# Two queues for the K and V loads of a decode attention kernel: each load split by columns, the second half issued by ScalarE

## The chip, the cores and the metric

One core of a Trainium2 chip. The time is device microseconds (us) of one execution of the whole kernel, from inputs in the chip's main memory to the output in it. Three runs of the kernel before took 1362.27, 1363.26 and 1363.33 us; the median is 1363.26.

The engines named here: PE (TensorE, matrix products), DVE (VectorE), ACT (ScalarE), POOL (GpSimd) and SP (SyncE, which here only issues transfers). Transfers run on 16 transfer (DMA) engines that all queues share. A transfer is cut into packets, here one for each partition's row, and every transfer engine carries the rows of 8 of the 128 partitions and then one 4-byte packet that counts up the transfer's semaphore.

## The reference

One token is decoded. Attention over a cache of 16384 positions in 32 heads, beside a gated GELU block, both on the normalised input, all in float32:

```python
def _A_ref(x, k_cache, v_cache, wq, wo):              # H, Dh = 32, 128; D = 576
    q = (x @ wq).reshape(B, Sq, H, Dh).transpose(0, 2, 1, 3)
    scores = jnp.einsum("bhqd,bhkd->bhqk", q, k_cache) * (Dh ** -0.5)
    p = _softmax(scores, axis=-1)                       # 16384 keys a head
    o = jnp.einsum("bhqk,bhkd->bhqd", p, v_cache)
    return o.transpose(0, 2, 1, 3).reshape(B, Sq, H * Dh) @ wo

def _B_ref(x, w_gate, w_up, w_down):                    # 576 -> 4608 -> 576
    g, u = x @ w_gate, x @ w_up
    return (_gelu(g) * u) @ w_down

x = A_x
xn = _layernorm(x, axis=-1)
return x + _A_ref(xn, ...) + _B_ref(xn, ...)
```

K and V of one head are 16384 x 128 floats each, 8.39 MB; 32 heads make 537 MB of the 587.6 MB that the kernel reads.

## The kernel before

A head's K lies on the 128 partitions as 128 keys a partition, in one row of 65536 B (N * DH floats); so does its V. There are three places of that size: `kt[0]` (in the profile kb) for the even heads' K, `kt[1]` (ka) for the odd heads' K, and one `vt` for V.

The kernel opens with the projections: wq, w_gate and w_up are loaded and multiplied on DVE row by row. Then every engine runs its own program for the heads, and they meet through semaphores that `take` waits for and counts down again (line 118).

- DVE (`scores`, line 367) waits for K, multiplies it in place by the broadcast query (line 356), sums over the 128 columns of each key (line 360), releases the K place with `s_kf` (line 362) and forms the maximum over all keys (lines 363 and 365).
- PE (`on_pe`, line 332) makes the broadcast query of the next head but one, transposes and spreads the maximum, waits for the exponentials and for V (`s_v`, line 341), and multiplies both in 32 products (line 344). After ACT has copied the sums it brings them into a column (line 349), and the first of these products releases V's place with `s_vf` (line 351).
- ACT (`on_act`, line 385), one loop over pairs of heads, copies the query, takes the exponentials (line 395), copies PE's sums (line 397) and the head's column (line 399).
- SP (`on_sp`, line 417) issues the loads, all on its one queue, in the order K of head 2, V of head 1, K of head 3, V of head 2 and so on: each waits until its place is released.

K of head 0 comes in two loads by columns (lines 411 and 412), every other K and V in one. After SP's loop follow, on the same queue and in this order: the first part of w_down into kb's place (`wd0`, 28 blocks of 576, line 427, when head 30's K is done with), V of head 31 (line 428, when V's place is released by head 30), the second part of w_down (line 429) and the first part of wo (both when head 31's K is done with), and the second part of wo into kb's place again (line 445), which waits for `k_w0`, the last of the 28 multiply-adds of wd0.

At the end DVE adds w_down's blocks into `wacc` (line 253, 28 from wd0, then 8), normalises the heads' outputs (lines 462 to 469), adds 11 blocks of wo, and sums its part with that of PE (line 495); PE does the rest of wo, ACT and DVE copy the row out and SP writes it.

Of the kernel before, what the change touches and what calls it, by code (L numbers as in the profile page):

```python
# [8 lines left out]
AF = mybir.ActivationFunctionType  # L9
# [5 lines left out]
H, SK, DH = 32, 16384, 128  # L15
D, DF = 576, 4608
N = SK // P
DJ = 4
DM = P * DJ
SCALE = DH**-0.5  # L20
# [18 lines left out]
class Plan:  # L39
# [24 lines left out]
    def dma(self, e, out, in_, *deps, sem=None):  # L64
        sem = sem or self.sem(f"d{len(self.count)}")
        return self.op(e, lambda g: g.dma_start(out, in_), *deps, sig=sem, by=16)
# [51 lines left out]
def take(g, sem, n=1):  # L118
    g.wait_ge(sem, n).then_inc(sem, -n)  # L119
# [12 lines left out]
def plan(nc, pl, x, k_cache, v_cache, wq, wo, wg, wu, wd, out):  # L132
    op, dma = pl.op, pl.dma
    kv = k_cache.rearrange("b h (p n) d -> (b h) p (n d)", p=P)
    vv = v_cache.rearrange("b h (p n) d -> (b h) p (n d)", p=P)
# [8 lines left out]
    def small(name, shape, where=None):  # L144
        if where is None:
            size = 4
            for n in shape[1:]:
                size *= n
            where = place[name] = top[0]
            top[0] += -(-size // 32) * 32  # L150
            assert top[0] <= S0, (name, top)
        return nc.alloc_sbuf_tensor_at(name, shape, F32, offset=where).ap()

    def big(name, floats, where):
        assert where + 4 * floats <= 3 * SLOT
        return nc.alloc_sbuf_tensor_at(name, [P, floats], F32, offset=S0 + where).ap()
# [8 lines left out]
    qb = [small(f"qb{i}", [P, DH]) for i in range(2)]  # L165
    sc = [small(f"sc{i}", [P, N]) for i in range(2)]
    pm, nm, nb, pe = small("pm", [P, 1]), small("nm", [1, 1]), small("nb", [P, 1]), small("pe", [P, N])
    ls, o4 = small("ls", [P, H + 1]), small("o4", [P, 512])
    oall, oT = small("oall", [P, H + 1]), small("oT", [P, WT])
# [15 lines left out]
    kt = [big("kb", N * DH, B), big("ka", N * DH, A)]  # L185
    vt = big("vt", N * DH, C)
# [4 lines left out]
    def banks(*shapes):  # L191
        with ExitStack() as s:
            return [s.enter_context(nc.psum_tensor(n, [P, b, 512], F32)).ap() for n, b in shapes]

    (pw,) = banks(("pw", 3))
    pt, pb, pc, pqb, po, acc, fin = banks(("pt", 1), ("pb", 1), ("pc", 1), ("pqb", 1), ("po", 1), ("acc", 2), ("fin", 1))
    px = pc[:, 0, :]

    s_hs, s_pm, s_nm, s_p, s_o4, s_v = (pl.sem(n) for n in ("hs", "pm", "nm", "p", "o4", "v"))
    s_pq, s_pt, s_pb, s_pv, s_pc = (pl.sem(n) for n in ("pq", "pt", "pb", "pv", "pc"))  # L200
    s_qb, s_ol, s_kf, s_vf, s_d, s_a = (pl.sem(n) for n in ("qb", "ol", "kf", "vf", "d", "a"))
    s_kh, s_aside = pl.sem("kh"), pl.sem("aside")
    s_k = [pl.sem(f"k{i}") for i in range(2)]
# [44 lines left out]
    s_r, s_w, s_h0, s_q0 = (pl.sem(n) for n in ("r", "w", "h0", "q0"))  # L248
# [12 lines left out]
    def rows(w, t, d, parts, between=None):  # L261
        n = w[0].shape[-1] // 2
        r = [u[:, j * n : (j + 1) * n] for u in w for j in range(2)]
        op("dve", lambda g: g.tensor_scalar(r[0], r[0], xp[:, :1], None, op0=ALU.mult), d[0], k_x)
        add(r[1], r[1], xp[:, 1:2], r[0])
        made = between and between()
        for i in range(2):
            c = r[1][:, i * n // 2 : (i + 1) * n // 2]
            add(c, t, xt[:, i : i + 1], c, d[1])
        k_s = add(r[2], r[2], xp[:, 2:3], r[1], d[2])  # L270
        v = [u.rearrange("p (i c) -> p i c", i=4) for u in (r[3], r[2])]
        for lo, hi, to in parts:
            k = add(bv[:, :, to : to + hi - lo], v[0][:, :, lo:hi], xp[:, 3:4], v[1][:, :, lo:hi])
        pads = [op("pool", lambda g, lo=lo, hi=hi: g.memset(bv[:, :, lo:hi], 0.0), k_s)
                for lo, hi in ((384, SEL), (SEL + 384, 2 * SEL), (2 * SEL + 256, 3 * SEL)) if len(parts) > 1]
        pl.then("dve", [s_r], k, *pads[-1:])
        return k_s, k, made
# [25 lines left out]
    def pick(g, h):  # L303
        return g.activation(hsel, hcol[:, bass.ds(h, 1)].to_broadcast([P, P]), AF.Copy)  # L304
# [5 lines left out]
    u_k, _, k_g = rows(uw, ut, d_u, [(0, DF // 4, 0)], lambda: select(gu[:, 0], SEL, 32, 2))  # L310
# [11 lines left out]
    v = sel[:, : 32 * FT].rearrange("p (r t) -> p r t", r=32)  # L322
    k = op("pool", lambda g: g.tensor_mul(v, v, m32[:, :32].unsqueeze(2).to_broadcast([P, 32, FT])), k, c_m32)
    for r in (16, 8, 4, 2, 1):
        o = v[:, :r, :] if r > 1 else u_.unsqueeze(1)
# [6 lines left out]
    def on_pe(g):  # L332
        with g.Fori(0, H):
            take(g, s_hs)
            g.matmul(pqb[:, 0, :DH], hsel, qsel, start=True, stop=True).then_inc(s_pq, 1)  # L335
            take(g, s_pm)
            g.transpose(pt[:1, 0, :P], pm, ident).then_inc(s_pt, 1)  # L337
            take(g, s_nm)
            g.matmul(pb[:, 0, :1], ones[:1, :], nm, start=True, stop=True).then_inc(s_pb, 1)  # L339
            take(g, s_p)  # L340
            take(g, s_v, 16)
            for k in range(0, N, 4):
                q = 32 * (k // 4 % 4)
                m = g.matmul(po[q : q + 4, 0, :], pe[:, k : k + 4], vt[:, k * DH : (k + 4) * DH],  # L344
                             start=k < 16, stop=k >= N - 16)
            m.then_inc(s_pv, 1)
            take(g, s_o4)
            for j in range(4):
                m = g.matmul(pc[:, 0, :1], o4[:, j * DH : (j + 1) * DH], m32[:, j : j + 1], start=j == 0, stop=j == 3)  # L349
                if j == 0:  # L350
                    m.then_inc(s_vf, 1)
            m.then_inc(s_pc, 1)

    def products(g, i, n=(0, N)):
        kd = kt[i].rearrange("p (n d) -> p n d", d=DH)[:, n[0] : n[1], :]
        g.tensor_mul(kd, kd, qb[i].unsqueeze(1).to_broadcast([P, n[1] - n[0], DH])).then_inc(s_d, 1)  # L356
        take(g, s_d)
# [7 lines left out]
        g.tensor_reduce(nm, pt[:1, 0, :P], axis=AX.X, op=ALU.max, negate=True).then_inc(s_nm, 1)  # L365

    def scores(g, i):
        take(g, s_k[i], 16)
        take(g, s_qb)
        products(g, i)  # L370
        sums(g, i)

    def on_dve(g):
# [7 lines left out]
        with g.Fori(0, H // 2 - 1):  # L381
            for i in range(2):
                scores(g, i)

    def on_act(g):
        with g.Fori(0, H, 2) as h2:
            for i in range(2):
                h = h2 + i
                take(g, s_pq)
                g.activation(qb[1 - i], pqb[:, 0, :DH], AF.Copy).then_inc(s_qb, 1)  # L390
                pick(g, h + 2).then_inc(s_hs, 1)
                take(g, s_pb)
                g.activation(nb, pb[:, 0, :1], AF.Copy, scale=SCALE).then_inc(s_a, 1)  # L393
                take(g, s_a)
                g.activation(pe, sc[i], AF.Exp, bias=nb, scale=SCALE, accum_out=ls[:, bass.ds(h, 1)]).then_inc(s_p, 1)  # L395
                take(g, s_pv)
                g.activation(o4, po[:, 0, :], AF.Copy).then_inc(s_o4, 1)  # L397
                take(g, s_pc)
                g.activation(oall[:, bass.ds(h, 1)], pc[:, 0, :1], AF.Copy).then_inc(s_ol, 1)

    pl.call("pe", on_pe)
    pl.call("dve", on_dve)
    pl.call("act", on_act)

    def load_k(h, *deps):
        dma("sp", kt[h % 2], kv[h], *deps, sem=s_k[h % 2])

    def load_v(h):
        dma("sp", vt, vv[h], (s_vf, 1) if h else (s_w, 3), sem=s_v)

    dma("sp", kt[0][:, : N // 2 * DH], kv[0][:, : N // 2 * DH], g_k, sem=s_kh)
    dma("sp", kt[0][:, N // 2 * DH :], kv[0][:, N // 2 * DH :], sem=s_k[0])
    load_k(1, u_k)
    load_v(0)
    two = [c.rearrange("(m t) p f -> t m p f", t=2) for c in (kv, vv)]

    def on_sp(g):
        with g.Fori(0, H // 2 - 1) as m:
            for i in range(2):
                take(g, s_kf)  # L420
                g.dma_start(kt[i], two[0][i, bass.ds(m + 1, 1)].rearrange("o p f -> (o p) f")).then_inc(s_k[i], 16)
                take(g, s_vf)
                v = two[1][1, bass.ds(m, 1)] if i == 0 else two[1][0, bass.ds(m + 1, 1)]
                g.dma_start(vt, v.rearrange("o p f -> (o p) f")).then_inc(s_v, 16)

    pl.call("sp", on_sp)
    d_wd0 = dma("sp", wd0, wdv[:, : WD1 * D], (s_kf, 1))
    load_v(H - 1)
    d_wd1 = dma("sp", wd1, wdv[:, WD1 * D :], (s_kf, 2))
    k_o = s_ol, H  # L430

# [12 lines left out]
    for n in WO_CUTS:  # L444
        w, base, dep = (wo0, 0, (s_kf, 2)) if lo < WO1 else (wo1, WO1, k_w0)
        c = w[:, (lo - base) * D : (lo - base + n) * D]
# [3 lines left out]
        if lo == WO1:  # L450
            last = wo.rearrange("(s r t) f -> t r s f", s=2, t=WT)[WT - 1]
            for r in [b + j for b in (0, 32) for j in range(4)]:
                to = aside[r : r + 29 : 4].rearrange("r (s f) -> r s f", s=2)
                d_aside = dma("sp", to, last[r : r + 29 : 4, :, LEFT:], dep, sem=s_aside)
    assert len(d_wo) == WT - 2
    for t, a, b in ((WT - 2, LEFT, D), (WT - 2, 0, LEFT), (WT - 1, 0, LEFT)):
        c = wo1[:, (t - WO1) * D + a : (t - WO1) * D + b]
# [12 lines left out]
    for t in ON_DVE:  # L470
        for i, c in enumerate((oT[: P // 2, WT - 1 :], o31) if t == ASIDE else ()):
            to = o_sum[: P // 2, LEFT:]
# [35 lines left out]
    to = osb.rearrange("o a f -> o (a f)")  # L508
    c = op("act", lambda g: g.activation(to[:, LEFT:], third, AF.Copy), k2)
# [31 lines left out]
```

## Time and profile before

| | |
|---|---|
| median of three runs | 1363.26 us (1362.27 to 1363.33) |
| span of the profiled execution, first to last instruction | 1360.5 us |
| DVE busy | 1243.5 us (91%) |
| PE busy | 391.3 us (29%) |
| ACT busy | 66.9 us (5%) |
| transfer engines busy (SP's queue) | 99.8% |
| read from main memory | 587.60 MB, 432 GB/s over the span |

The profiled execution is known by its span; what lies around it in the device time is the 2.8 us between the span and the median of the runs, if it ran like them.

How the rows further down are read. A row of the timeline has the start and the duration in us, the engine, the line of the kernel, the operation, out<-in by the program's names, shapes and count, and in brackets the idle time of the engine before it and what ended it (DVEq is DVE's own sequencer, waiting at a semaphore). SPq is SP issuing a transfer. A row of landings has out<-in, the issuing queue, the count, the KB of each where they are given, and the median us from issue to landing. A row that begins with q1, q8 or q14 counts a hardware queue's packets that start in the given window: packets, MB, and the time that these packets took as a share of 16 engines in the window. In a narrow window one packet's time is therefore share x window x 16. q1 is SP's queue; q8 and q14 bring instructions.

### The profile page before, as it was taken

How to read it: one execution, taken by the hardware profiler on the slowest of the kernel's cores; microseconds unless marked ns; L12 is line 12 of the kernel's file. 1: busy time of each engine (PE TensorE's matmuls, PEld its weight loads, DVE VectorE, ACT ScalarE, POOL GpSimd, SP SyncE). 2: the span in 40 equal slices, each digit the busy share in tenths (PEclk: the TensorE clock that was granted, in tenths of full speed). 3: DMA queues.
4: the chain of work that ended last, by engine and by line, in shares of the span. 5: the costliest groups of instructions: out<-in, count | busy, mean ns of one | idle time of the engine just before them, and what ended most of it. 6: DMA issues, size and time to landing. Idle time of an engine off the chain costs nothing. (4 is left out here: it accounts for less than half of the span.)

```text
span 1360.5 us, 6992 instructions
## 1 busy us (share of the span) xinstructions
PE 391.3 (29%) x2650; PEld 122.4 (9%) x2650; DVE 1243.5 (91%) x228; ACT 66.9 (5%) x234; POOL 36.0 (3%) x25
## 2 busy tenths in 40 slices
PE   0211233333211333333222333332223333322136
PEld 0000011001000111100000111010001111000011
DVE  7999999999988888898888888998888889988888
ACT  0000000000000000000000000000000000000000
POOL 0063000000000000000000000000000000000000
PEclk9655666666556666666556666655666666655667
DMA  9999999999999999999999999999999999999998
GB/s 405 429 437 432 434 447 441 432 432 432 434 432 434 432 432 432 435 451 435 432 432 432 434 432 434 432 432 432 441 447 434 432 432 434 432 434 432 431 432 374
DMA packets 12870, 587.63 MB, mean 432 GB/s; under 512 B 1474, under 2 KB 1986, under 8 KB 2756
## 3 DMA queue, kind: packets, MB, share of 16 engines
q1 hardware_dynamic: 12866, 587.60, 99.8%
q8 instruction: 1, 0.02, 0.0%
q10 hardware_dynamic: 2, 0.00, 0.0%
q14 instruction: 1, 0.01, 0.0%
HBM read 587.60 MB, written 0.00 MB: 432 GB/s over the span
## 5 line engine op out<-in xcount | busy, mean ns | idle before, releaser
L344 PE MATMUL po<-vt,pe 128*4 128x512 f32 x2048 | 291.8, 733 | 611.5 <-PEq L119 611.5
L356 DVE TENSOR_TENSOR kb<-kb,qb 128x16384 f32<-128x16384 f32 (+1 forms) x17 | 277.3, 16314 | 31.8 <-DVEq L119 31.8
L356 DVE TENSOR_TENSOR ka<-ka,qb 128x16384 f32<-128x16384 f32 x16 | 275.6, 17226 | 32.1 <-DVEq L119 32.1
L360 DVE TENSOR_REDUCE sc<-kb 128x128 f32<-128x16384 f32 x16 | 275.5, 17220 | 2.3
L360 DVE TENSOR_REDUCE sc<-ka 128x128 f32<-128x16384 f32 x16 | 275.5, 17220 | 2.3
L344 PEld LDWEIGHTS po<-vt,pe 128*4 128x4 f32 x2048 | 56.3, 98 | 819.9 <-issue 819.9
L337 PE MATMUL pt<-ident,pm 128*1 128x128 f32 x32 | 11.9, 372 | 223.1 <-PEq L119 223.1
L397 ACT ACTIVATE o<-po 128x512 f32<-128x512 f32 x32 | 19.1, 597 | 877.1 <-ACTq L119 877.1
L349 PE MATMUL pc<-m,o 128*128 128x1 f32 x256 | 32.7, 249 | 28.9 <-PEq L119 28.9
L349 PEld LDWEIGHTS pc<-m,o 128*128 128x128 f32 x256 | 31.0, 191 | 57.8 <-issue 57.8
L253 DVE SCALAR_TENSOR_TENSOR wacc<-wd,hT,wacc 128x576 f32<-128x576 f32 x36 | 29.5, 819 | 4.1 <-DMA wd<-in_B_w_down_dram 2.9
L286 PE MATMUL pw<-both,ones 128*32 128x396 f32 x72 | 11.5, 801 | 63.3 <-PEq L119 63.3
L365 DVE TENSOR_REDUCE nm<-pt 1x1 f32<-1x128 f32 x32 | 8.9, 278 | 21.5 <-DVEq L119 21.5
L337 PEld LDWEIGHTS pt<-ident,pm 128*1 128x1 f32 x32 | 2.5, 79 | 228.2 <-issue 228.2
L339 PE MATMUL pb<-nm,ones 1*128 1x1 f32 x64 | 17.7, 343 | 18.5 <-PEq L119 18.5
L339 PEld LDWEIGHTS pb<-nm,ones 1*128 1x128 f32 x64 | 15.9, 307 | 27.8 <-issue 27.8
L393 ACT ACTIVATE nb<-pb 128x1 f32<-128x1 f32 x32 | 5.5, 171 | 254.1 <-ACTq L119 254.1
L363 DVE TENSOR_REDUCE pm<-sc 128x1 f32<-128x128 f32 x32 | 9.2, 286 | 7.6 <-DVEq L119 7.6
L335 PE MATMUL pqb<-qsel,hsel 128*128 128x128 f32 x64 | 14.9, 315 | 1.8 <-PEq L119 1.8
L395 ACT ACTIVATE pe<-sc,nb 128x128 f32<-128x128 f32 x32 | 12.8, 401 | 6.1 <-ACTq L119 6.1
L304 ACT ACTIVATE hsel<-hcol 128x128 f32 (+1 forms) x34 | 10.2, 301 | 41.3 <-DVE qsel L297 41.2
L326 POOL TENSOR_TENSOR tmp<-tmp 128x576 f32<-128x576 f32 (+3 forms) x4 | 11.3, 2836 | 0.3
(93 smaller groups left out, 177.9 us busy)
## 6 DMA issues: line engine op xcount, KB each, us to landing
g<-in_B_w_gate_dram SPq DMA_DIRECT2D x2, 4608.0 KB, 39.5
u<-in_B_w_up_dram SPq DMA_DIRECT2D x2, 4608.0 KB, 32.3
q<-in_A_wq_dram SPq DMA_DIRECT2D x2, 4096.0 KB, 17.4
kb<-in_A_k_cache_dram SPq DMA_DIRECT2D x2, 4096.0 KB, 26.7
wd<-in_B_w_down_dram SPq DMA_DIRECT2D x1, 8064.0 KB, 42.0
wo<-in_A_wo_dram SPq DMA_DIRECT2D x1, 3456.0 KB, 35.9
wo<-in_A_wo_dram SPq DMA_DIRECT2D x2, 1728.0 KB, 28.6
wd<-in_B_w_down_dram SPq DMA_DIRECT2D x1, 2304.0 KB, 28.1
```

The lines of the kernel that those rows point to most:

```text
L253: return op("dve", lambda g: g.scalar_tensor_tensor(out, w, c, into, op0=ALU.mult, op1=ALU.add), *deps)
L286: m = g.matmul(pw[32 * i : 32 * i + 32, b, :SEL], ones[:, :32], bv[:, i, b * SEL : (b + 1) * SEL], start=True, stop=True)
L326: k = op("pool", lambda g, o=o, r=r: g.tensor_tensor(o, v[:, :r, :], v[:, r : 2 * r, :], op=ALU.add), k)
L335: g.matmul(pqb[:, 0, :DH], hsel, qsel, start=True, stop=True).then_inc(s_pq, 1)
L337: g.transpose(pt[:1, 0, :P], pm, ident).then_inc(s_pt, 1)
L339: g.matmul(pb[:, 0, :1], ones[:1, :], nm, start=True, stop=True).then_inc(s_pb, 1)
L344: m = g.matmul(po[q : q + 4, 0, :], pe[:, k : k + 4], vt[:, k * DH : (k + 4) * DH], start=k < 16, stop=k >= N - 16)
L349: m = g.matmul(pc[:, 0, :1], o4[:, j * DH : (j + 1) * DH], m32[:, j : j + 1], start=j == 0, stop=j == 3)
L356: g.tensor_mul(kd, kd, qb[i].unsqueeze(1).to_broadcast([P, n[1] - n[0], DH])).then_inc(s_d, 1)
L360: g.tensor_reduce(sc[i], kt[i].rearrange("p (n d) -> p n d", d=DH), axis=AX.X, op=ALU.add).then_inc(s_d, 1)
L395: g.activation(pe, sc[i], AF.Exp, bias=nb, scale=SCALE, accum_out=ls[:, bass.ds(h, 1)]).then_inc(s_p, 1)
L397: g.activation(o4, po[:, 0, :], AF.Copy).then_inc(s_o4, 1)
```

## The change

Each load of K and V after the first head's K becomes two, of columns 0 to 8191 and 8192 to 16383 (`halves`; 32768 B a partition each), on the same semaphore, for which DVE and PE now wait until 32. SP issues the first half where it issued the whole. The second half is issued by ACT, on ACT's own queue: K's right after the exponentials of the head whose place it takes, V's right after the copy of PE's sums. Neither waits for `s_kf` or `s_vf` itself, since the instruction ahead of it on ACT comes after the last reader. K of head 1 and V of head 0 are also split, but both halves stay on SP. ACT's last two heads are written out behind its loop, because no K is left to load there; V of head 31 has its first half on SP behind wd0 and its second half on ACT.

```diff
@@ PE
-            take(g, s_v, 16)
+            take(g, s_v, 32)
@@ DVE
-        take(g, s_k[i], 16)
+        take(g, s_k[i], 32)
@@ ACT
+    halves = [slice(0, N // 2 * DH), slice(N // 2 * DH, N * DH)]
+
+    def half(g, to, sem, src, m, j):
+        src = src[bass.ds(m, 1)].rearrange("o p f -> (o p) f")
+        g.dma_start(to[:, halves[j]], src[:, halves[j]]).then_inc(sem, 16)
+
+    def next_k(g, m, i, j):
+        half(g, kt[i], s_k[i], two[0][i], m + 1, j)
+
+    def next_v(g, m, i, j):
+        half(g, vt, s_v, two[1][1 - i], m + i, j)
+
+    def head(g, h, i, m, k_too, v_too):
...
+        g.activation(pe, sc[i], AF.Exp, bias=nb, scale=SCALE, accum_out=ls[:, bass.ds(h, 1)]).then_inc(s_p, 1)
+        if k_too:
+            next_k(g, m, i, 1)
+        take(g, s_pv)
+        g.activation(o4, po[:, 0, :], AF.Copy).then_inc(s_o4, 1)
+        if v_too:
+            next_v(g, m, i, 1)
...
-        with g.Fori(0, H, 2) as h2:
+        with g.Fori(0, H // 2 - 1) as m:
             for i in range(2):
...
+                head(g, m * 2 + i, i, m, True, True)
+        for i in range(2):
+            head(g, H - 2 + i, i, H // 2 - 1, False, i == 0)
@@ SP
-    load_k(1, u_k)
-    load_v(0)
+    load(kt[1], kv[1], s_k[1], u_k)
+    load(vt, vv[0], s_v, (s_w, 3))
...
                 take(g, s_kf)
-                g.dma_start(kt[i], two[0][i, bass.ds(m + 1, 1)].rearrange("o p f -> (o p) f")).then_inc(s_k[i], 16)
+                next_k(g, m, i, 0)
                 take(g, s_vf)
...
+                next_v(g, m, i, 0)
...
-    load_v(H - 1)
+    dma("sp", vt[:, halves[0]], vv[H - 1][:, halves[0]], (s_vf, 1), sem=s_v)
```

On SP, in the loop over the heads and just behind it, the queue has these rows (- before, + after; kb and ka are the places of K, vt that of V, wd_111 the first part of w_down):

```order
-L421 DMA kb<-in_A_k_cache_dram 128x16384
-L424 ISA
-L424 DMA vt<-in_A_v_cache_dram 128x16384
-L421 ISA
-L421 DMA ka<-in_A_k_cache_dram 128x16384
-L424 DMA vt<-in_A_v_cache_dram 128x16384
...
+L390 DMA kb<-in_A_k_cache_dram 128x8192
+L390 ISA
+L390 DMA vt<-in_A_v_cache_dram 128x8192
+L390 ISA
+L390 DMA ka<-in_A_k_cache_dram 128x8192
+L390 DMA vt<-in_A_v_cache_dram 128x8192
```

The order is the same; each load has half the columns.

On ACT, in the first half of a pass of its loop, the rows after are these (sc is a head's scores, po PE's sums):

```order
L400 ACTIVATE qb_72<-pqb 128x128
L304 ISA
L304 ACTIVATE hsel<-hcol 128x128
L403 ACTIVATE nb<-pb 128x1
L405 ISA
L405 ACTIVATE pe,ls<-sc_73,nb 128x128
L390 ISA
L390 DMA kb<-in_A_k_cache_dram 128x8192
L409 ACTIVATE o_80<-po 128x512
L390 ISA
L390 DMA vt<-in_A_v_cache_dram 128x8192
```

Two transfers now stand between ACT's own instructions, one behind the exponentials and one behind the copy of the sums.

Behind SP's loop its queue differs in one row (wd_111 and wd_112 are the two parts of w_down, wo_113 the first part of wo, vt the V of head 31):

```order
+L436 COMPARE_AND_BRANCH
 L66 DMA wd_111<-in_B_w_down_dram 128x16128
-L66 DMA vt<-in_A_v_cache_dram 128x16384
+L66 DMA vt<-in_A_v_cache_dram 128x8192
 L66 DMA wd_112<-in_B_w_down_dram 128x4608
 L66 DMA wo_113<-in_A_wo_dram 128x6912
```

The other half of that V is in ACT's program for head 30, behind its loop:

```order
+L403 ACTIVATE nb<-pb 128x1
+L405 ACTIVATE pe,ls<-sc_73,nb 128x128
+L409 ACTIVATE o_80<-po 128x512
+L390 DMA vt<-in_A_v_cache_dram 128x8192
+L413 ACTIVATE oall<-pc 128x1
```

Before, the whole V of head 31 stood on SP's queue between the two parts of w_down; now one half stands there, and the other is on ACT's queue.

## Rows read from the trace of the kernel before

**Rows 1.** The page: busy times, SP's queue, and the chain by lines.

```profile
PE 391.3 (29%) x2650; PEld 122.4 (9%) x2650; DVE 1243.5 (91%) x228; ACT 66.9 (5%) x234; POOL 36.0 (3%) x25
...
q1 hardware_dynamic: 12866, 587.60, 99.8%
...
DMA wd<-in_B_w_down_dram 2%; DVE wacc L253 1%; PE fin L478 0%; DVE part L495 0%; DVE oT L468 0%; DVE rl L462 0%; PE pt L465 0%; DVE ot L466 0%; DVE oexp L463 0%; ACT osb L511 0%; DVE o L469 0%; DVEq L87 0%; DVEq L362 0%
```

**Rows 2.** Timeline of ACT and DVE, heads in the middle, and head 31.

```profile
606.30 0.60 ACT L397 ACTIVATE o<-po 128x512 f32<-128x512 f32 x1 [29.38 <-ACTq L119]
...
615.40 0.19 ACT L395 ACTIVATION_READ_ACCUMULATOR pe<-sc,nb  x1
...
655.12 17.23 DVE L356 TENSOR_TENSOR ka<-ka,qb 128x16384 f32<-128x16384 f32 x1 [2.59 <-DVEq L119]
...
1273.32 17.23 DVE L356 TENSOR_TENSOR ka<-ka,qb 128x16384 f32<-128x16384 f32 x1 [2.59 <-DVEq L119]
```

**Rows 3.** Timeline of SP's issues: the first, two in the middle, three late.

```profile
0.73 0.41 SPq L66 DMA_DIRECT2D q<-in_A_wq_dram  x1
...
607.63 0.33 SPq L424 DMA_DIRECT2D vt<-in_A_v_cache_dram  x1
...
612.82 0.33 SPq L421 DMA_DIRECT2D ka<-in_A_k_cache_dram  x1
...
1263.67 0.33 SPq L424 DMA_DIRECT2D vt<-in_A_v_cache_dram  x1
...
1269.43 0.34 SPq L66 DMA_DIRECT2D wd<-in_B_w_down_dram  x1
...
1335.32 14.68 SPq L66 DMA_DIRECT2D wo<-in_A_wo_dram  x10
```

**Rows 4.** Landings, us from issue, of those issued from 607.63 on, in order.

```profile
vt<-in_A_v_cache_dram SPq DMA_DIRECT2D x1, 27.9
...
ka<-in_A_k_cache_dram SPq DMA_DIRECT2D x1, 42.1
...
vt<-in_A_v_cache_dram SPq DMA_DIRECT2D x1, 28.7
...
wd<-in_B_w_down_dram SPq DMA_DIRECT2D x1, 8064.0 KB, 42.0
...
wo<-in_A_wo_dram SPq DMA_DIRECT2D x1, 1728.0 KB, 17.6
```

**Rows 5.** Packets starting in 620.34:620.36, 83.20:83.22, 83.28:83.30 and 1.7:1.8.

```profile
q1 hardware_dynamic: 1, 0.07, 755.6%
...
q1 hardware_dynamic: 1, 0.03, 379.1%
...
q1 hardware_dynamic: 1, 0.00, 2.8%
...
q1 hardware_dynamic: 3, 0.10, 350.1%
```

**Rows 6.** Packets in 83.36:83.38 (q14), 83.68:83.70, 141.16:141.18 (q8) and 142.08:142.10.

```profile
q14 instruction: 1, 0.01, 96.6%
...
q1 hardware_dynamic: 2, 0.03, 549.1%
...
q8 instruction: 1, 0.02, 291.2%
...
q1 hardware_dynamic: 1, 0.07, 911.2%
```

**Rows 7.** Timeline of PE, ACT and DVE at the end.

```profile
1292.51 7.81 PE L344 MATMUL po<-vt,pe 128*4 128x512 f32 x48 [21.07 <-PEq L119]
...
1302.20 0.60 ACT L397 ACTIVATE o<-po 128x512 f32<-128x512 f32 x1 [29.79 <-ACTq L119]
...
1311.41 23.88 DVE L253 SCALAR_TENSOR_TENSOR wacc<-wd,hT,wacc 128x576 f32<-128x576 f32 x28 [2.03 <-DMA wd<-in_B_w_down_dram]
...
1336.21 6.80 DVE L253 SCALAR_TENSOR_TENSOR wacc<-wd,hT,wacc 128x576 f32<-128x576 f32 x8 [0.92 <-DMA wd<-in_B_w_down_dram]
```

More of the change, by code (lines that the diff above doesn't have):

```diff
@@ L383, in on_dve @@
                 scores(g, i)
+    two = [c.rearrange("(m t) p f -> t m p f", t=2) for c in (kv, vv)]
+    halves = [slice(0, N // 2 * DH), slice(N // 2 * DH, N * DH)]
[7 more added lines that the diff above has]
+    def head(g, h, i, m, k_too, v_too):
+        take(g, s_pq)
+        g.activation(qb[1 - i], pqb[:, 0, :DH], AF.Copy).then_inc(s_qb, 1)
+        pick(g, h + 2).then_inc(s_hs, 1)
+        take(g, s_pb)
+        g.activation(nb, pb[:, 0, :1], AF.Copy, scale=SCALE).then_inc(s_a, 1)
+        take(g, s_a)
+        g.activation(pe, sc[i], AF.Exp, bias=nb, scale=SCALE, accum_out=ls[:, bass.ds(h, 1)]).then_inc(s_p, 1)
[5 more added lines that the diff above has]
+            next_v(g, m, i, 1)
+        take(g, s_pc)
+        g.activation(oall[:, bass.ds(h, 1)], pc[:, 0, :1], AF.Copy).then_inc(s_ol, 1)
     def on_act(g):
-        with g.Fori(0, H, 2) as h2:
+        with g.Fori(0, H // 2 - 1) as m:
             for i in range(2):
[L388 to L399, printed above, removed]
+                head(g, m * 2 + i, i, m, True, True)
+        for i in range(2):
+            head(g, H - 2 + i, i, H // 2 - 1, False, i == 0)
     pl.call("pe", on_pe)
@@ L403, in plan, with load @@
     pl.call("act", on_act)
[L405 to L409, printed above, removed]
+    def load(to, src, sem, *deps):
+        for c in halves:
+            dma("sp", to[:, c], src[:, c], *deps, sem=sem)
     dma("sp", kt[0][:, : N // 2 * DH], kv[0][:, : N // 2 * DH], g_k, sem=s_kh)
     dma("sp", kt[0][:, N // 2 * DH :], kv[0][:, N // 2 * DH :], sem=s_k[0])
-    load_k(1, u_k)
-    load_v(0)
-    two = [c.rearrange("(m t) p f -> t m p f", t=2) for c in (kv, vv)]
+    load(kt[1], kv[1], s_k[1], u_k)
+    load(vt, vv[0], s_v, (s_w, 3))
     def on_sp(g):
@@ L420, in on_sp @@
                 take(g, s_kf)
-                g.dma_start(kt[i], two[0][i, bass.ds(m + 1, 1)].rearrange("o p f -> (o p) f")).then_inc(s_k[i], 16)
+                next_k(g, m, i, 0)
                 take(g, s_vf)
-                v = two[1][1, bass.ds(m, 1)] if i == 0 else two[1][0, bass.ds(m + 1, 1)]
-                g.dma_start(vt, v.rearrange("o p f -> (o p) f")).then_inc(s_v, 16)
+                next_v(g, m, i, 0)
     pl.call("sp", on_sp)
     d_wd0 = dma("sp", wd0, wdv[:, : WD1 * D], (s_kf, 1))
-    load_v(H - 1)
+    dma("sp", vt[:, halves[0]], vv[H - 1][:, halves[0]], (s_vf, 1), sem=s_v)
     d_wd1 = dma("sp", wd1, wdv[:, WD1 * D :], (s_kf, 2))
```

## The prediction

> **What bounds the kernel now.** I read the page first, for busy shares, the transfer engines and the chain of waits [rows 1], then the timeline of a head in the middle with the issues and landing times of its loads [rows 2 to 4], then single packets [rows 5, 6], and last the timeline of the final 70 us [rows 7].
>
> The page shows VectorE busy for 91% of the span, yet the one hardware queue in use keeps the 16 transfer engines busy for 99.8% of it [rows 1]. Which of the two sets the pace is seen in the middle: VectorE waits 2.59 us ahead of every product [rows 2], and that wait ends when K lands: K is issued at 612.82 and takes 42.1 us, so it is there at 654.9, and the product starts at 655.12 [rows 2 to 4]. Two such starts 16 heads apart (655.12 and 1273.32) give 618.20 / 16 = 38.64 us a head, 19.32 us for each of its two loads of 128 x 65536 B, or 434 GB/s. The stream never runs dry: V is issued at 607.63 and lands after 27.9 us, of which 19.3 is its own passage, so 8.6 us of other work still lie ahead of it; ahead of K lie 42.1 - 19.3 = 22.8 us [rows 3, 4]. The middle is therefore priced by what a packet costs, not by when a load is issued.
>
> At the end it is otherwise. The chain of waits that ended last leaves the transfers with w_down and goes on through VectorE's multiply-adds of line 253 [rows 1]. Followed back from there: the first part of w_down lands at 1269.43 + 42.0 = 1311.43, its 28 multiply-adds start at 1311.41 and last 23.88 us to 1335.29; VectorE waits 0.92 us for the second part, and from 1336.21 on the chain is VectorE's (with one PE transpose inside it) up to the sum of the parts, line 495, then PE, ScalarE and the output [rows 1, 3, 4, 7]. So a later landing of the first part moves the end by all but 0.92 us of its delay.
>
> **What the change does, and its price.** The sum is made against the profiled span, 1360.5 us; the median of the runs shown is 1363.26, 2.8 us more, which I keep as it is.
>
> *More packets.* A row of 65536 B becomes two of 32768 B. Of single packets, 7.556 x 0.02 us x 16 engines = 2.418 us for the large one and 3.791 x 0.32 = 1.213 us for the small one, so two small ones take 2.426, 0.008 more [rows 5]. Packets overlap a little: a load passes in 19.32 us, or 2.414 a row after its semaphore packet, 0.004 less than 2.418. With that overlap for the added packet too, 0.004 us net a row. Each engine has 8 rows of a load, and 63 loads are split (31 of K, 32 of V): 504 x 0.004 = 2.0 us. Each split adds a semaphore packet of 0.028 x 0.32 = 0.009 us [rows 5], 0.005 after overlap: 63 x 0.005 = 0.3. With rounding I take +2.5 us. No cover: the engines are the bound.
>
> *Two queues at once.* No stretch of the trace has two busy queues, so this is bounded by the nearest rows. From below: if the second queue hid the whole fixed cost of a packet (0.008 us), the 504 rows would lose what they now pay, 4.1 us gained instead of 2.5 lost. From above: two isolated packets of instruction queues cut into the stream. After the one on q14 the next row took 5.491 x 0.32 - 0.009 = 1.748 us instead of 1.213, 0.535 more; the one on q8, of 16384 B, took 2.912 x 0.32 = 0.932 us where twice the 8192 B packet is 0.62, and the next large row 9.112 x 0.32 = 2.916 instead of 2.418 [rows 5, 6]. Of the 63 split loads 61 run on both queues (all but K of head 1 and V of head 0): at 0.535 for each of their 61 x 16 = 976 packets that is +522 us. These are lone packets that break into a running queue; two queues that both always have the next row ready are nearer to one queue whose rows follow each other at 2.414 us. I take 0, and keep both ends.
>
> *Who goes first.* From the start of the loop the queues run side by side. ScalarE's half of K is issued about 2.8 us after SP's (after the accumulator read that follows the exponential, 615.40 + 0.19, against 612.82) [rows 2, 3] and its half of V about 0.7 us before (606.30 + 0.60 against 607.63) [rows 2, 3]. A shift of one row or two between them delays each landing by as much, once; with 22.8 and 8.6 us in the queue this does not starve the engines. ScalarE is 5% busy and a DMA issue takes about 0.33 us [rows 1, 3]; it stands after the exponential and after the copy of the sums, while PE works on, so I cost it at nothing. Were the cover gone, 0.33 x 61 = 20 us would be the price.
>
> *The end.* Here order costs time. Before, the queue holds V of head 30, then the first part of w_down, then V of head 31 (line 428). After, V's second half for head 31 is on ScalarE's queue, which is empty by then, so it does not wait behind w_down: it takes turns with it. V of head 30 lands at 1263.67 + 28.7 = 1292.37; PE starts on it at 1292.51 and ScalarE's copy ends at 1302.20 + 0.60 = 1302.80 [rows 3, 4, 7]. A first packet follows its issue by about 1.0 us (the kernel's first issue stands at 0.73, its first three packets between 1.7 and 1.8) [rows 3, 5], so V's rows arrive at about 1303.9. The first part of w_down passes in 1311.43 - 1292.37 = 19.06 us, eight rows of 2.38; by 1303.9 nearly five of them are through. Turn by turn, a row of V (1.21 us) then goes ahead of each of the rest. The packet on q14 shows the grain: it stands between the last row of a load and that load's semaphore packet, which follows at 83.68 to 83.70 in front of the slow row [rows 6]. So two or three rows of w_down and its semaphore are each held back: 2 to 4 x 1.21 = 2.4 to 4.8 us. I take three, 3.6 us; 0.92 us is absorbed, so the end moves by 2.7 (1.5 to 3.9). V of head 31 itself lands as before, since the bytes up to it are the same. What is late next is the release of the second half of wo (line 445), which waits for the last of the 28 multiply-adds: issued at 1335.32, landing after 17.6 us, of which 1728 KB at 434 GB/s are 4.1, so 13.5 us of other work lie ahead of it, and it can come 3.6 us later [rows 3, 4].
>
> Sum: 1360.5 + 2.5 + 2.7 = 1365.7 of span, and 1363.26 + 5.2 = **1368.5 us**.
>
> **Rivals.**
> 1. *Whole shares in turn.* If an engine sends all rows of one DMA before it looks at the other queue, V's half for head 31 waits until w_down is through, and the end moves by the packets alone: 1363.26 + 2.5 = 1365.8. For it: nothing else has ever shared the engines for long. Against it: the q14 packet came ahead of the load's own semaphore packet [rows 6]. The Trainium skill (DMA: Bandwidth & Descriptors, "Queues, rings and completion order") has the engines turn round-robin at packet boundaries, with some 9 to 17 descriptors in a packet; eight rows and a semaphore would be one packet, which is this rival. The q14 row does not agree with it for this queue.
> 2. *The queues hide each other's gaps.* The fixed cost vanishes: -4.1 us, and with the order of rival 1 at the end 1363.26 - 4.1 = 1359.2, faster than before; with the 2.7 of my forecast 1361.9, no change. For it: there is a gap a packet to hide. Against it: packet times grow by a constant with the engine already at one speed, so the gap sits in the engine, which both queues share; and the tail's chain on VectorE starts from landings that the gain must reach. It decides only if more than two thirds of the fixed cost goes.
> 3. *Each turn costs.* A tenth of the 0.535 us at every one of 976 turns gives +52 us, 1363.26 + 52 + 5 = 1420; all of it 1363.26 + 522 + 5 = 1890. For it: both lone packets show it [rows 6], and the kernel's first three rows, sent into an empty pipe, took 3.501 x 0.1 x 16 / 3 = 1.87 us each instead of 1.21 [rows 5]. Against it: these are first packets after a pause, not alternation. It decides from about 10 ns a turn.
>
> That the split does not happen can be excluded: the order of instructions shows each DMA at 128 x 8192.
>
> **Chances.** Forecast 0.5 (its own range 1366 to 1372), rival 1 0.22, rival 2 0.13 (0.05 of it faster), rival 3 0.15. About 0.2%, 2.7 us, is what a measurement of this kernel can tell from no change: faster is below 1360.5, slower above 1366.0. Faster holds rival 2's better half, 0.05. Same holds the rest of rival 2, 0.08, most of rival 1, 0.17, and the forecast's edge, 0.06: 0.31. Slower holds the rest, 0.64. The range for 8 in 10 leaves out most of rival 3 and the faster half of rival 2: 1361 to 1376, where 1376 also takes in turns of up to about 8 ns.
>
> **What would show it.** In the profile after: two hardware queues with near equal bytes; the middle period at 38.64 + 0.08 us a head; packets of 32768 B that each appear longer, since two are under way, with the sum unchanged; the first part of w_down issued at about the same place and landing some 3.6 us later against V of head 30, with the 28 multiply-adds ending after the second part has landed (no 0.92 us wait); the chain still on VectorE to the end. A period above 39 us would prove rival 3, one below 38.6 rival 2, and an unmoved landing of w_down rival 1.

## The result and the profile after

The changed kernel takes 1367.74 us (median of six, 1366.61 to 1370.03) against 1363.30 for the kernel before in the same runs: 4.4 us or 0.36% slower, ratio 1.0036 (95% interval 1.0026 to 1.0046). The forecast was 1368.5. The profiled execution took 1367.68 us, of which the span is 1364.9, 4.4 us more than before.

The page of the changed kernel, its queues and its chain of waits by lines, answers to [rows 1]:

```profile
q1 hardware_dynamic: 13154, 331.75, 56.4%
q10 hardware_dynamic: 8786, 255.86, 43.4%
...
DMA wd<-in_B_w_down_dram 3%; DVE wacc L253 3%; PE fin L495 0%; DVE part L512 0%; PE pt L482 0%; DVE oT L485 0%; DVE rl L479 0%; ACT osb L526 0%; DVE oexp L480 0%; DVE ot L483 0%; ACT osb L528 0%; DVE o L486 0%; DVEq L87 0%; DVEq L362 0%; ACTq L87 0%
```

ACT's queue (q10) now carries 44% of the bytes, and the two queues together keep the engines as busy as one did (99.8% in both). The chain still leaves the transfers with w_down, and DVE's share of it has grown from 1% to 3%: its 28 multiply-adds for the first part of w_down have joined it.

In the middle, the timeline of DVE (start, duration, the idle time ahead in brackets) answers to [rows 2], and the packets of 200 to 1200 us, with a single one of 620.34 to 620.36 (q10) and of 620.66 to 620.68 (q1), answer to [rows 5]:

```profile
657.56 17.23 DVE L356 TENSOR_TENSOR ka<-ka,qb 128x16384 f32<-128x16384 f32 x1 [2.67 <-DVEq L119]
...
1277.14 17.23 DVE L356 TENSOR_TENSOR ka<-ka,qb 128x16384 f32<-128x16384 f32 x1 [2.65 <-DVEq L119]
```

```profile
q1 hardware_dynamic: 7441, 216.57, 50.2%
q10 hardware_dynamic: 7440, 216.53, 50.1%
...
q10 hardware_dynamic: 1, 0.03, 379.1%
...
q1 hardware_dynamic: 1, 0.03, 379.1%
```

The period is (1277.14 - 657.56) / 16 = 38.72 us a head where it was 38.64. A packet takes 3.791 x 0.32 = 1.213 us on either queue, to the digit what a packet of this size took alone on one queue [rows 5]; the two queues share the engines exactly by halves. 433.1 MB pass in 1000 us; before it was 434.2, in the same view: `q1 hardware_dynamic: 7457, 434.18, 100.2%`.

At the end, the timeline of PE, ACT, SP and DVE answers to [rows 3, 7]:

```profile
1297.60 8.88 PE L344 MATMUL po<-vt,pe 128*4 128x512 f32 x64 [22.41 <-PEq L119]
...
1306.64 0.60 ACT L409 ACTIVATE o<-po 128x512 f32<-128x512 f32 x1 [30.54 <-ACTq L119]
1306.66 0.35 ACTq L390 DMA_DIRECT2D vt<-in_A_v_cache_dram  x1
...
1316.52 30.78 DVE L253 SCALAR_TENSOR_TENSOR wacc<-wd,hT,wacc 128x576 f32<-128x576 f32 x36 [3.31 <-DMA wd<-in_B_w_down_dram]
...
1360.19 0.76 DVE L512 TENSOR_TENSOR part<-acc,wacc 128x576 f32<-128x576 f32 x1
```

The 28 multiply-adds start at 1316.52 instead of 1311.41, 5.1 us later, and run into the next 8 without the wait of 0.92 us: one row of 36 where there were two. The sum of the parts moves from 1355.76 to 1360.19, by the 4.4 us of the result; in the kernel before it stood here:

```profile
1355.76 0.76 DVE L495 TENSOR_TENSOR part<-acc,wacc 128x576 f32<-128x576 f32 x1
```

Two places in the trace show where a turn of the other queue came in. First the packets of the changed kernel in 1292.9 to 1294.7, then 1294.7 to 1297.7, then 1306.7 to 1310.1 and 1310.1 to 1312.3:

```profile
q1 hardware_dynamic: 19, 0.97, 124.1%
q10 hardware_dynamic: 5, 0.07, 8.5%
...
q1 hardware_dynamic: 17, 1.10, 84.3%
q10 hardware_dynamic: 13, 0.00, 0.2%
...
q1 hardware_dynamic: 25, 1.61, 109.4%
...
q1 hardware_dynamic: 6, 0.39, 40.6%
q10 hardware_dynamic: 10, 0.33, 34.5%
```

In the second stretch ACT's queue has nothing left of V of head 30 but 13 semaphore packets (0.00 MB), and they pass among 17 rows of w_down: each waits its turn behind a row of 2.38 us. PE therefore sees V of head 30 at 1297.60. In the third stretch there is no packet of ACT's queue, though V of head 31 was issued at 1306.66; its rows come from 1310.1 on, 3.5 us after the issue. It is not the end of a running row that they wait for: 25 rows of w_down begin in that stretch, on 16 engines. From 1310.1 on, six of the engines carry a row of V ahead of w_down's last row and another ahead of its semaphore packet, two turns; on the other ten the last row had already begun, and only the semaphore packet waits. The engine that ends last is one of the six, and the landing goes by it.

### The profile page after: what moved, and what is told of

It is laid out like the page before. It is cut to its first block, busy times and chain, and to the rows that moved or that the text cites. A ratio compares the mean times of both kernels' runs of the same rounds, so it can differ in the third digit from the quotient of the medians.

```text
span 1364.9 us, 7153 instructions
## 1 busy us (share of the span) xinstructions
PE 389.5 (29%) x2650; PEld 122.6 (9%) x2650; DVE 1243.5 (91%) x228; ACT 66.9 (5%) x234; POOL 35.9 (3%) x25
```

## The experiments

Two theories to begin with. *Packets and turns*: some 2.7 us are the packets that the split adds, on whatever queue; the rest is the end, where w_down's last row and its semaphore each wait for a row of V on ACT's queue. *Two queues*: the turns between two queues cost the middle its time. A third, for the end alone: the shift between the queues, which counts V of head 30 late, and not the place of V of head 31.

Beside these kernels the kernel before took 1362.4 to 1362.6 us, 0.8 to 0.9 less than beside the changed kernel, so what is compared with the expectations is the difference to the kernel before, not the time.

**One queue.** Both halves of each load stay on SP; ACT's loop is that of before.

```diff
                 take(g, s_kf)
-                next_k(g, m, i, 0)
+                for j in range(len(halves)):
+                    next_k(g, m, i, j)
                 take(g, s_vf)
-                next_v(g, m, i, 0)
+                for j in range(len(halves)):
+                    next_v(g, m, i, j)
```

> The split without the second queue: both halves of every load on SP, one behind the other, ACT issues none. Packet theory (2.7 us of the 4.4 are the added packets, on whatever queue; the rest is the end, where w_down's last row and its semaphore each wait for a row of V on ACT's queue): period 38.72 us a head as in the changed kernel, the end as before with VectorE waiting 0.9 us between the two parts of w_down, 1363.3 + 2.7 = 1366.0 us. Rival, turns between two queues cost the middle its time: period 38.64, 1363.3 to 1363.6 us.

1365.38 us (11 runs) against 1362.55, ratio 1.0020 (1.0011 to 1.0029): 2.8 us. The timeline of this kernel's DVE and PE:

```profile
656.32 17.22 DVE L356 TENSOR_TENSOR ka<-ka,qb 128x16384 f32<-128x16384 f32 x1 [2.67 <-DVEq L119]
...
1275.91 17.23 DVE L356 TENSOR_TENSOR ka<-ka,qb 128x16384 f32<-128x16384 f32 x1 [2.65 <-DVEq L119]
```

```profile
1295.19 5.04 PE L344 MATMUL po<-vt,pe 128*4 128x512 f32 x24 [21.24 <-PEq L119]
...
1314.09 23.88 DVE L253 SCALAR_TENSOR_TENSOR wacc<-wd,hT,wacc 128x576 f32<-128x576 f32 x28 [2.12 <-DMA wd<-in_B_w_down_dram]
1338.94 6.80 DVE L253 SCALAR_TENSOR_TENSOR wacc<-wd,hT,wacc 128x576 f32<-128x576 f32 x8 [0.96 <-DMA wd<-in_B_w_down_dram]
```

The period is 619.59 / 16 = 38.72 us, that of the changed kernel to 0.01. So the middle's loss belongs to the split, and the second queue neither adds to it nor takes from it. V of head 30 and w_down both come 2.7 us later than before (1295.19 and 1314.09 against 1292.51 and 1311.41), and the wait of 0.96 us is there again.

**V of head 31 on SP.** The changed kernel, but ACT issues nothing for head 31.

```diff
-            head(g, H - 2 + i, i, H // 2 - 1, False, i == 0)
+            head(g, H - 2 + i, i, H // 2 - 1, False, False)
...
-    dma("sp", vt[:, halves[0]], vv[H - 1][:, halves[0]], (s_vf, 1), sem=s_v)
+    load(vt, vv[H - 1], s_v, (s_vf, 1))
```

> The changed kernel with both halves of head 31's V on SP behind the first part of w_down; all else on two queues. Packet theory with the end as told: period 38.72, V of head 30 still counted as landed late because ACT's semaphore packet waits out a row of w_down, but w_down itself lands only 2.7 us later than before (1314.1), 1366.0 us. Rival, the late count of V of head 30 or the shift between the queues is what costs the end: 1367.7 us as in the changed kernel.

1365.64 us (11 runs) against 1362.55, ratio 1.0019 (1.0009 to 1.0028): 3.1 us. PE and DVE in this kernel:

```profile
1297.58 9.60 PE L344 MATMUL po<-vt,pe 128*4 128x512 f32 x64 [22.41 <-PEq L119]
...
1314.11 23.88 DVE L253 SCALAR_TENSOR_TENSOR wacc<-wd,hT,wacc 128x576 f32<-128x576 f32 x28 [0.90 <-DMA wd<-in_B_w_down_dram]
```

V of head 30 is as late as in the changed kernel (1297.58), 2.4 us later than on one queue, and it costs nothing: w_down starts at 1314.11, as with one queue. So the late count of V of head 30 is not what moves the end; the 2.41 us between 1314.11 and 1316.52 come with the one load that ACT no longer issues here.

**The end alone.** The kernel before, but ACT issues the second half of V of head 31 (PE's last head is written out, since it waits for two loads).

```diff
+        if v_too:
+            g.dma_start(vt[:, halves[1]], vv[H - 1][:, halves[1]]).then_inc(s_v, 16)
...
-    load_v(H - 1)
+    dma("sp", vt[:, halves[0]], vv[H - 1][:, halves[0]], (s_vf, 1), sem=s_v)
```

> The kernel before, whole loads on one queue, but for head 31's V, of which ACT issues the second half (PE's last head is written out behind its loop). Theory: two or three turns of 1.21 us ahead of w_down's last rows and semaphore, w_down lands at 1313.8 to 1315.0 instead of 1311.4, 0.9 is absorbed: 1364.8 to 1366.0 us. Rival, the end of the changed kernel is late for the shift between the queues and not for this load: 1363.3 us.

1365.89 us (11 runs) against 1362.55, ratio 1.0025 (1.0016 to 1.0034): 3.3 us for half of one load among 64. DVE and ACT's issue in this kernel, then a row of the kernel before:

```profile
1290.94 17.22 DVE L364 TENSOR_REDUCE sc<-ka 128x128 f32<-128x16384 f32 x1
...
1301.67 0.38 ACTq L402 DMA_DIRECT2D vt<-in_A_v_cache_dram  x1
...
1315.29 30.79 DVE L253 SCALAR_TENSOR_TENSOR wacc<-wd,hT,wacc 128x576 f32<-128x576 f32 x36 [5.65 <-DMA wd<-in_B_w_down_dram]
```

```profile
1290.69 17.22 DVE L360 TENSOR_REDUCE sc<-ka 128x128 f32<-128x16384 f32 x1
```

The reduction of head 31 starts at 1290.94, 0.25 us later than in the trace of before (1290.69 there), w_down 3.88 us later. The difference, 3.63 us, is three turns of 1.21. Here V of head 30 has no semaphore on another queue, PE is on time, and V of head 31 comes early enough for one turn more than in the changed kernel. The 3.3 us (2.2 to 4.6 by the interval) lie above the 1.5 to 2.7 that were expected; three turns less the wait of 0.92 make 2.7, and the rest no run takes apart. The turns are counted in one profiled execution of each kernel; the eleven runs lie between 1364.97 and 1367.00 us.

**Whole loads on two queues.** K on SP, V on ACT, rows of 65536 B, V of head 31 on SP.

```diff
-    halves = [slice(0, N // 2 * DH), slice(N // 2 * DH, N * DH)]
+    halves = [slice(0, N * DH)]
...
-            next_k(g, m, i, 1)
+            pass
...
-            next_v(g, m, i, 1)
+            next_v(g, m, i, 0)
...
-                take(g, s_vf)
-                next_v(g, m, i, 0)
...
-    dma("sp", vt[:, halves[0]], vv[H - 1][:, halves[0]], (s_vf, 1), sem=s_v)
+    dma("sp", vt, vv[H - 1], (s_vf, H - 1), sem=s_v)
```

> Whole loads of 65536 B a row, K on SP's queue and V on ACT's (V of head 31 on SP), so two queues take turns but no packet is added. Packet theory: period 38.64 us a head as before, each packet 2.418 us; about 1363 us if the end is not moved by the other order of loads there. Rival, turns cost: period 38.7 or more, 1366 us or more.

1533.3 us (5 runs) against 1362.55, ratio 1.125 (1.1235 to 1.1265). The first expectation missed; the rival's 1366 us or more is met by its words alone, since the rows below show no cost of a turn. The kernel can't serve as the comparison of periods that it was meant for. Its packets in 640 to 660 us, then in 707 to 716, and a piece of its DVE and PE:

```profile
q1 hardware_dynamic: 64, 4.19, 48.4%
q10 hardware_dynamic: 64, 4.19, 48.4%
...
q10 hardware_dynamic: 16, 0.00, 0.1%
```

```profile
592.33 17.23 DVE L356 TENSOR_TENSOR kb<-kb,qb 128x16384 f32<-128x16384 f32 x1 [0.25 <-DVEq L119]
...
668.00 0.29 DVE L363 TENSOR_REDUCE pm<-sc 128x1 f32<-128x128 f32 x1 [0.24 <-DVEq L119]
668.45 9.58 PE L344 MATMUL po<-vt,pe 128*4 128x512 f32 x64 [34.70 <-PEq L119]
680.55 0.28 DVE L365 TENSOR_REDUCE nm<-pt 1x1 f32<-1x128 f32 x1 [12.27 <-DVEq L119]
681.07 17.23 DVE L356 TENSOR_TENSOR kb<-kb,qb 128x16384 f32<-128x16384 f32 x1 [0.25 <-DVEq L119]
```

Where both queues have work they go row for row, 64 and 64, at 0.484 x 20 x 16 / 64 = 2.42 us a packet, as on one queue: the turns are free here too. But K and V, now side by side, each pass at half speed, so V lands when the next head's K is done with. PE waits for it ahead of the transpose of the next maximum, DVE waits 12.27 us for that transpose, the K places come free late, and from 707 to 716 nothing moves but 16 semaphore packets. Two heads take 681.07 - 592.33 = 88.74 us, 44.37 a head and 5.7 more than before, which over some 30 heads is the 171 us. That this order of waits is the cause is read from the trace; no further run took it apart.

**Quarters.** As the one-queue kernel, with four loads of 16384 B a partition.

```diff
-    halves = [slice(0, N // 2 * DH), slice(N // 2 * DH, N * DH)]
+    halves = [slice(j * N // 4 * DH, (j + 1) * N // 4 * DH) for j in range(4)]
```

> Every load after the first head's K in four of 16384 B a partition, all on SP's one queue. Packet theory: three packets more a row instead of one, so three times the loss of the split in two on one queue: 3 x 2.8 = 8.4 us, a period of 38.64 + 0.26 = 38.90 us a head, 1371 us. Rival, the loss comes from having more than one transfer under way for a place and not from the count of packets: about 1365.4 us as with two halves.

1370.72 us (5 runs) against 1362.40, ratio 1.0060 (1.0047 to 1.0074): 8.3 us, 2.9 times the 2.8 of one cut for three times the added packets. In 200 to 1200 us this kernel moves 431.29 MB; a single packet of it, in 600.09 to 600.11:

```profile
q1 hardware_dynamic: 29607, 431.29, 100.7%
...
q1 hardware_dynamic: 1, 0.02, 190.9%
```

A row of 16384 B takes 1.909 x 0.32 = 0.611 us, so four take 2.444 where the whole row takes 2.418 and two halves 2.426: 0.026 us more instead of 0.008, the same threefold. The rival, 1365.4 us, fell.

**The end with short rows.** As "the end alone", but ACT issues its half in four pieces of 8192 B a partition.

```diff
-            g.dma_start(vt[:, halves[1]], vv[H - 1][:, halves[1]]).then_inc(s_v, 16)
+            for j in range(4):
+                c = slice((4 + j) * N // 8 * DH, (5 + j) * N // 8 * DH)
+                g.dma_start(vt[:, c], vv[H - 1][:, c]).then_inc(s_v, 16)
```

> As tail_only (whole loads on one queue, ACT issues the second half of head 31's V), but ACT issues this half in four pieces of 8192 B a partition. Theory (w_down's last rows and its semaphore each wait for one row of the other queue): three turns of 0.31 instead of 1.21 us, w_down lands about 0.9 us late instead of 3.6, the wait of 0.9 us before w_down's second part absorbs it: 0.0 to 0.5 us over the kernel before. Rival, a second queue takes a fixed share of the engines or costs a fixed time however short its rows: 3.3 us over it, as tail_only.

1379.11 us (4 runs) against 1362.40, ratio 1.0120 (1.0105 to 1.0136). The time is far from both expectations, the landing of w_down is the one expected. DVE and PE in this kernel, then its packets in 1325 to 1328, then PE's start on V of head 31 in the kernel before:

```profile
1312.59 30.78 DVE L253 SCALAR_TENSOR_TENSOR wacc<-wd,hT,wacc 128x576 f32<-128x576 f32 x36 [2.94 <-DMA wd<-in_B_w_down_dram]
...
1347.48 9.85 PE L343 MATMUL po<-vt,pe 128*4 128x512 f32 x64 [37.13 <-PEq L119]
...
1359.54 0.36 DVE L476 RECIPROCAL rl<-pqb 128x32 f32<-128x32 f32 x1 [16.17 <-PE pqb L475]
```

```profile
q1 hardware_dynamic: 48, 0.88, 68.6%
q10 hardware_dynamic: 48, 0.39, 30.9%
```

```profile
1330.88 9.12 PE L344 MATMUL po<-vt,pe 128*4 128x512 f32 x64 [20.80 <-PEq L119]
```

w_down starts at 1312.59, 1.2 us later than before instead of 3.9: its last rows waited for short rows only. What I had not reckoned with is the other side of the turn. ACT's queue gets one row for each row of SP's, 48 and 48 in this stretch, however short its own are. Its 32 rows of 8192 B an engine need as many turns, nearly all of them against rows of up to 32768 B, so V of head 31 is complete only when PE starts, at 1347.48 instead of 1330.88, and the end waits for PE (16.17 us on DVE).

No run points to a version faster than before: the second queue gives nothing in the middle, and in the three kernels that use it for V of head 31 it takes turns away from a queue that is already full.

## Why the prediction was right

*More packets.* Right in cause and nearly in size: 2.5 us forecast, 2.8 measured with one queue, and 38.72 us a head as forecast (38.64 + 0.08). The quarters show that the loss goes with the count of packets.

*Two queues at once.* Taken at 0, measured at 0: the period with two queues equals that with one. Rival 3 fell, and with it the reading of the lone packets as the price of a turn. What the slow rows behind those packets paid for stays open. It was not the breaking into a queue that is alone: in the end-alone kernel ACT's first row of V of head 31 breaks into SP's running queue, takes 3.791 x 0.32 = 1.213 us, and the row of w_down behind it takes 7.438 x 0.32 = 2.380, as undisturbed ones do (packets in 1305.10 to 1305.12 and 1306.31 to 1306.33):

```profile
q10 hardware_dynamic: 1, 0.03, 379.1%
...
q1 hardware_dynamic: 1, 0.06, 743.8%
```

Rival 2 fell too: nothing was hidden, 1.213 us a packet on either queue. ACT's issuing, costed at nothing, cost nothing either: the period is 38.72 us with its issues and without them.

*The end.* The mechanism was right: row for row, and the semaphore packet waits like a row. The end-alone experiment shows it by itself, with three turns. In the changed kernel there were two, so 2.4 us instead of the forecast's 3.6: 1316.52 - 1314.11. Less the absorbed wait of 0.95 this is 1.5 us where the forecast had 2.7, at the lower end that was given for it. Two steps of the working were wrong here. The first is a term that it had and priced at nothing, the shift between the queues: V of head 30 was taken to land at the same place in the queue as before, but ACT's semaphore packet for it waited out a row of w_down, and PE started 2.4 us later still. The second, "a first packet follows its issue by about 1.0 us", was read at the start, into empty engines; into full ones it took 3.4 us in the end-alone kernel (1301.67 to 1305.11) and 3.5 here. (0.6 of that was won back: the issue goes out with the start of ACT's copy, 1306.64, where the working had its end.) Both bring V of head 31 later and so take turns away. By the working's own figures, nearly five of eight rows through at 1303.9, three rows and the semaphore packet are left: four turns on the engine that ends last, not three. The late first packet alone left three (the end-alone kernel), the late count of V of head 30 with it two. With four the sum would have been 1369.7; that three was taken from the stated 2 to 4 is why the 1367.74 us came out only 0.8 below the forecast, and so far the closeness is luck.

*The signs.* The period, the lost wait of 0.92 us and the chain on DVE came as named. Three did not. The bytes are equal in the middle only, 56% to 44% over the whole kernel. The packets did not appear longer: 1.213 us on either queue, as alone. And w_down did not land later against V of head 30: 1316.52 - 1297.60 = 18.92 us, as before (1311.41 - 1292.51 = 18.90), since that landing slipped as well.

*Whole shares in turn* (rival 1) fell: 13 semaphore packets among 17 rows, and 64 rows against 64. The Trainium skill (DMA: Bandwidth & Descriptors, "Queues, rings and completion order") is borne out in the round-robin; its packet of some 9 to 17 descriptors is not what these queues show, where a turn is one row (64 against 64).

The sum, from the traces: 1311.41 + 2.68 (split, one queue) + 2.43 (two turns) = 1316.52 for w_down's landing; less 0.92 of wait and with the rest of the end unchanged to 0.3 us, 4.4 us.

## What to carry to other kernels

This is what the runs of one kernel show. Where the transfer engines are the bound and their packets already follow one another, a second issuing queue buys nothing, and each packet that a split adds is paid in full. Before a load is moved to another queue, look at what it will then take turns with: turns go row for row whatever the rows' lengths, semaphore packets wait like rows, so a landing on the critical chain slips by the other queue's row, and a load in short rows beside one in long rows starves. Two streams of which one is needed first belong on one queue in that order, or each cut evenly over both.

## What the runs showed of the hardware that was not expected

That a 4-byte semaphore packet waits its turn like a row was forecast for w_down; not expected was that it also holds up a load whose rows are all through: ACT's half of V of head 30 was counted 2.4 us late, behind a row of w_down. Between the issue of a load on an idle queue and its first row lay 3.4 to 3.5 us while the other queue was full, against 1.0 us into empty engines; why, no run shows. As forecast, but shown by no row before, two queues that are both always full are as fast as one: 433.10 MB in 1000 us against 433.13 for the same packets on one queue:

```profile
q1 hardware_dynamic: 14868, 433.13, 100.3%
```
